# Retention attention and two mixtures of experts on one core: where weight halves are split around the last picks, one couple's transposes ahead of a weight copy, and the last block scaled by one engine

## The chip, the cores and the metric

The kernel runs on one NeuronCore of a Trainium2 chip. The metric is the device time of one execution in microseconds (us); lower is better. The engines are named as in the profile: PE (TensorE, the matrix multiplier; PEld is its loading of stationary operands), DVE (VectorE), ACT (ScalarE), POOL (GpSimd) and SP (SyncE, which here only issues DMAs). Each engine works through its own instructions in the order in which the program issues them.

## The reference, cut to what matters

```python
x = attention(q, k, v)                       # (2, 8, 768, 64) -> 1536 tokens x 512, decayed state per head
# first layer of experts: tokens with a positive skip score, top 1 of 8
xc = x[x @ w_skip > 0];  logits = xc @ w_gate;  e_idx = argmax(logits)
gate_w = softmax(logits)[e_idx]
for e in range(8):                           # w1[e]: 512 x 1024, w2[e]: 1024 x 512
    y[mask] = gate_w[mask, None] * (relu(xc[mask] @ w1[e]) @ w2[e])
x[do_compute] = xc + y
# second layer: every token, top 1 of 8 again, with a capacity of 384 tokens for an expert
logits = x @ w_gate2;  expert_idx = argmax(logits)
out[i] = gate_w[i] * expert(expert_idx[i], x[i]) if kept else 0
```

## The kernel before, in words

Everything is float32 at the interface. A weight chunk (128 x 2048, 1 MB) is loaded by SP into one of five raw buffers `big` and then **split in halves**: for each half ACT writes `hi` (a rounded copy, line 252) and DVE writes `lo` (the rest, line 255), both 128 x 1024. PE then multiplies `hi` and `lo` parts separately, three matmuls for one product (lines 786 to 788 and 794). A raw buffer is free for the next load when `lo` of its second half is done. The chunks come in a fixed order: for the first layer `w1a`, `w2a` of experts 0 to 7, then `w1b`, `w2b` of experts 0 to 7. Up to eleven halves can be held ready.

The schedule is written by hand. PE's stream is a row of steps, and after most of them the program calls `step_side()`. That moves the generators in the list `side` one step on and then calls `pump(1, pieces[0])`, which splits at most `pieces[0]` halves and issues what loads can start. `site()` moves the generators in the list `sited` one step on. So the number in `pieces[0]` decides beside which step a half is split, and the order of `site()` and `step_side()` decides what stands first on ACT and DVE.

In the first layer the loop runs over the experts `e`: `layer1` of expert `e` (x @ w1a, eight groups of matmuls into `s`), `layer2` of expert `e-1` (into `o`), and in between `turned`, which transposes on PE (line 765) into a buffer `t` and splits the result over ACT and DVE (lines 378 and 379: `xh`, `xl`, or `hTh`, `hTl`). There are three buffers `t`, used in turn, so a transposing step waits until the one three places before it has been read by both engines.

When an expert's rows are done (`result`, line 849, writes `row`), its tokens must be routed to the second layer's experts. `route_b` does that for the couples (0, 1), (2, 3) and (4, 5), for expert 6 and for expert 7. Its steps: transpose the rows (PE line 870, ACT copies `x2t`, line 871); logits (PE line 875, ACT `lgs`); the **pick** on DVE (`mx`, `d`, `t`, `tm`, `m`, lines 301 to 317); PE ranks the picked tokens (line 329); DVE makes of the ranks the slots and a one-hot matrix (`prb`, `slb`, `whereb`, lines 901 to 907); PE adds the tokens' numbers into the table `tab` (line 343).

Expert 7's pick is the last one, and it runs while PE does block (0, 0), the first 128 tokens of the second layer's expert 0, whose rows have been fetched before. Its thirteen small steps are numbered `i`; expert 7's `route_b` is moved on at `i` in (2, 4, 5, 8, 12), and at every third `i` there is a `step_side()`. Then DVE casts `tab` to `ids_b` (line 1078), and POOL gathers with it the rows of the next blocks from DRAM by indirect DMAs (line 362), block (0, 1) first. PE transposes that block's rows into `x` (line 765, `rowc`) inside `layer2` of block (0, 0). Before the change nothing is split in this stretch: `pieces[0]` is 0 there.

After that each expert has two blocks of 128 tokens, worked as a pair (lines 786 to 788). `emit_out` scales a finished block by the gate (line 919, `y`) and scatters it to the output by an indirect DMA (line 924). For the very last block alone ACT scales the left half and DVE the right half (line 921).

Of the kernel before, what the change touches and what calls it, by code (L numbers as in the profile page):

```python
# [11 lines left out]
ACTF = mybir.ActivationFunctionType  # L12
ALU = mybir.AluOpType
# [3 lines left out]
NT, DM, E, FF = B * S, H * D, 8, 1024  # L17
# [7 lines left out]
GCOL, IDCOL = DM, DM + 2  # L25
# [16 lines left out]
def kernel(  # L42
# [12 lines left out]
    nc = tc.nc  # L55
# [130 lines left out]
    def whole(kind, e, j):  # L186

        return kind == "w2a" and e in (1, 3) and j == 1
# [81 lines left out]
    def pump(n, pieces):  # L270

        count["turn"] += 1
        for _ in range(pieces):
            if not splitting:
                if not ready():
                    break
                splitting.append(split_half(n))
            try:
                next(splitting[0])
            except StopIteration:  # L280
                splitting.clear()
        load_w()
# [74 lines left out]
    def gather(at, n=None, t=None):  # L357

        n = n or done[0]
        if t is None:  # L360
            t = xs_free.pop(0)
        nc.gpsimd.indirect_dma_start(
            out=t, out_offset=None, in_=table[0:n, :], in_offset=bass.IndirectOffsetOnAxis(ap=at, axis=0),
            bounds_check=n - 1, oob_is_err=False,
        )
        return t
# [378 lines left out]
    def psum(tag="t", bufs=3):  # L745
        return ps.tile([128, 512], F32, tag=tag, bufs=bufs, name=tag)
# [13 lines left out]
    def turned(src, g, tag, divided=True):  # L760

        pool = x_p if tag == "x" else m_p
        t = psum()
        for k in range(4):
            nc.tensor.transpose(t[:, 128 * k:128 * k + 128], src[:, 512 * g + 128 * k:512 * g + 128 * k + 128], ident)
        t = t.rearrange("p (k t) -> p k t", k=4)
        if divided:
            w = 128 if tag == "x" else 256
            hi = pool.tile([128, 4, w], F32R, tag=tag + "h", name=tag + "h")[:, :, 0:128]
            lo = pool.tile([128, 4, w], F32R, tag=tag + "l", name=tag + "l")[:, :, 0:128]  # L770
            split(t, hi, lo)
            return hi, lo
        as_is = pool.tile([128, 4, 128], F32, tag=tag + "w", name=tag + "w", bufs=1)
        nc.scalar.activation(out=as_is, in_=t, func=ACTF.Copy)
        return (as_is,)

    def split_T(src, n, tag, divided=(True, True)):
        parts = []
        for g in range(n // 4):
            parts.append(turned(src, g, tag, divided[g]))  # L780
            yield
        return parts

    def mm3(acc, a, w, first, last):

        nc.tensor.matmul(out=acc, lhsT=a[0], rhs=w[0], start=first, stop=False)  # L786
        nc.tensor.matmul(out=acc, lhsT=a[0], rhs=w[1], start=False, stop=False)  # L787
        nc.tensor.matmul(out=acc, lhsT=a[1], rhs=w[0], start=False, stop=last)  # L788
# [12 lines left out]
    def layer1(x, kind, e, parts=None, fine=False):  # L801

        h = m_p.tile([128, FF], F32, tag="h", name="h", bufs=1)
        for j in range(2):
            acc = psum("s", 2)
            for k in (0, 2):
                w = wt[kind, e, j][k // 2]
                for _ in mm3s(acc, [(at_k(x, k + i), at_k(w, i)) for i in range(2)], k == 0, k == 2):
                    if fine:
                        yield  # L810
                if done_with(kind, e):
                    used((kind, e, j), k // 2)
                if not k:
                    if j and parts is not None:
                        parts.append(turned(h, 0, "hT"))
                    yield
            nc.scalar.activation(out=h[:, 512 * j:512 * j + 512], in_=acc, func=ACTF.Relu)
            yield
        return h
# [93 lines left out]
            to_slots(where[i], rhs[:, i], 8, 8)  # L913
        yield

    def emit_out(xs, acc, shared=False):
        y = m_p.tile([128, DM], F32, tag="y", name="y")
        n = DM // 2 if shared else DM
        nc.scalar.activation(out=y[:, 0:n], in_=acc[:, 0:n], func=ACTF.Copy, scale=xs[:, GCOL + 1:GCOL + 2])  # L919
        if shared:  # L920
            nc.vector.tensor_scalar(out=y[:, n:DM], in0=acc[:, n:DM], scalar1=xs[:, GCOL + 1:GCOL + 2], scalar2=None, op0=ALU.mult)  # L921
        ix = sm.tile([128, 1], I32, tag="ixo", name="ixo")
        nc.gpsimd.tensor_scalar(out=ix, in0=xs[:, IDCOL:IDCOL + 1], scalar1=4096.0, scalar2=None, op0=ALU.add)
        new = nc.gpsimd.indirect_dma_start(  # L924
            out=out[:, :], out_offset=bass.IndirectOffsetOnAxis(ap=ix, axis=0), in_=y, in_offset=None,
            bounds_check=NT - 1, oob_is_err=False,
        )
        for old in written:
            tc.declare_no_dep(new.ins, old.ins, reason="rows of other tokens")
        written.append(new)  # L930
        if xs is not a0:
            xs_free.append(xs)
# [18 lines left out]
    pieces = [1]  # L951

    def site():

        for g in list(sited):
            try:
                next(g)
            except StopIteration:
                sited.remove(g)

    def step_side():
        for g in list(side):
            try:
                next(g)
            except StopIteration:
                side.remove(g)
        pump(1, pieces[0])

    def run(gen):

        while True:
            try:
                next(gen)
            except StopIteration as stop:
                return stop.value
            step_side()
# [5 lines left out]
    def last_step(gen, n):  # L982

        for i in range(n):
            next(gen)
            if i < n - 1:
                step_side()
        try:
            next(gen)
        except StopIteration as stop:  # L990
            return stop.value

    def then_route(e, acc, between=lambda: None):

        result(e, xs1[e], acc)
        between()
        if e % 2 and e < E - 2:
            sited.append(route_b([e - 1, e], 1, 0))
        elif e == E - 2:
            side.append(route_b([e], 0, 0))  # L1000
# [15 lines left out]
    acc = run(second)  # L1016
    then_route(0, acc)
    for e in range(1, E):
        first = layer1(x, "w1a", e)
        if e == 1:  # L1020
            for _ in range(2):
                next(first)
                step_side()
            x = turned(xs1[2], 0, "x")
        h = run(first)
        if e + 4 < E:
            xs1[e + 4] = gather(ids[:, e + 4:e + 5], 1 + NT)
        elif e == 4:
            gather(ids[:, 8:9], 1 + NT, a0)
        turn = split_T(h, FT, "hT", (True, not whole("w2a", e, 1)))  # L1030
        if e > 1:
            second = layer2(hT.pop(e - 1), "w2a", e - 1)
            next(second)
            step_side()
            site()
            x = turned(xs1[e + 1] if e + 1 < E else a0, 0, "x")
            if e == E - 1:

                for _ in range(2):
                    next(second)  # L1040
                    step_side()
                    site()
                    next(turn)
            acc = last_step(second, FT // 2 - (3 if e == E - 1 else 1))
            then_route(e - 1, acc, step_side)
        if e < E - 1:
            site()
        hT[e] = run(turn)
    side += sited
    second = layer2(hT.pop(E - 1), "w2a", E - 1)  # L1050
    for i in range(FT // 2):
        next(second)
        pieces[0] = i < 2
        if i < FT // 2 - 1:
            step_side()
    acc = run(second)
# [4 lines left out]
    xs2 = {(0, 0): a0}  # L1061
# [6 lines left out]
    for i in range(1, 13):  # L1068
        next(first)
        if i % 3 == 0:  # L1070
            step_side()
        if i in (2, 4, 5, 8, 12):
            next(last)
# [14 lines left out]
    acc = run(second)  # L1088
# [44 lines left out]
    def pair_layer2(hs, e):  # L1133
        acc = [psum("o", 2), psum("o", 2)]
        for c in range(2):
            w = wt["w2b", e, c]
            for j in range(2):
                for k in range(4):
                    mm3(acc[j], at_k(hs[c], k, slice(128 * j, 128 * j + 128)), at_k(w[k // 2], k % 2), c + k == 0, c + k == 4)
                if c:  # L1140
                    emit_out(xs2[e, j], acc[j], e == E - 1 and j > 0)
                for h in range(2 * j):
                    used(("w2b", e, c), h)
                step_side()
# [11 lines left out]
    acc = run(second)  # L1156
# [207 lines left out]
```

## Time and profile before

| | |
|---|---|
| median of 3 runs | 385.44 us (385.2 to 385.46) |
| the profiled execution | 384.92 us |
| its span, first to last instruction | 383.1 us |
| PE busy | 368.7 us, 96% of the span |
| DVE, ACT, POOL busy | 64%, 56%, 32% |
| mean granted TensorE clock | 0.995 |

The profile is of one execution. The times in its rows count from the start of the span. Busy shares are means over stages with different limits: attention up to some 75 us, the first layer's experts up to some 190 us, the second layer's after that.

### The profile page before, as it was taken

Reading aid. Unit: us, or ns where it says so; the run is one execution under the profiler, and the core shown is the slowest. Engines: PE = TensorE matmul, PEld = TensorE weight load, DVE = VectorE, ACT = ScalarE, POOL = GpSimd, SP = SyncE. Lnnn points to the kernel's source line nnn. Section 1 sums busy time; section 2 is a strip of 40 time slices with the busy share of each in tenths; the row PEclk is TensorE's granted clock in tenths of the full one; section 3 lists DMA queues with packets and bytes.
Section 4 is the critical chain, followed back from the end, with each engine's and each line's share of the span. In section 5 each row is a group of like instructions: output and inputs, shape, how many; then the busy total and the mean of one; then the engine's idle time right before and its main releaser. Section 6 shows DMA issues by size and latency. Waiting matters only on the chain. (4 is left out here: it accounts for less than half of the span.)

```text
span 383.1 us, 6796 instructions
## 1 busy us (share of the span) xinstructions
PE 368.7 (96%) x2641; PEld 311.0 (81%) x2642; DVE 244.7 (64%) x402; ACT 213.8 (56%) x317; POOL 121.1 (32%) x185
## 2 busy tenths in 40 slices
PE   8999999799999999999999999999999999999992
PEld 4788887587777787886678998989899898998981
DVE  3657786479896999899626982747627466473200
ACT  1446554387986777795338763646546454562110
POOL 2677773285042060233251402205031140401102
PEclk9999999999999999999999999999999999999998
DMA  8999976689999999988746784947748386110001
GB/s 292 423 418 399 357 216 230 190 316 379 394 390 397 372 342 350 344 298 323 275 117 188 256 323 150 322 162 216 285 143 307 110 289 242 60 44 28 26 3 43
DMA packets 18128, 95.99 MB, mean 251 GB/s; under 512 B 2401, under 2 KB 2657, under 8 KB 8616
## 3 DMA queue, kind: packets, MB, share of 16 engines
q1 hardware_dynamic: 12196, 80.85, 57.2%
q0 software_dynamic: 3280, 9.76, 8.1%
q10 hardware_dynamic: 2612, 4.86, 3.5%
q8 instruction: 23, 0.38, 0.4%
q14 instruction: 17, 0.14, 0.1%
HBM read 87.03 MB, written 9.48 MB: 252 GB/s over the span
## 5 line engine op out<-in xcount | busy, mean ns | idle before, releaser
L255 DVE TENSOR_TENSOR lo<-big,hi 128x1024 fp32r<-128x1024 f32 (+1 forms) x130 | 151.3, 1185 | 54.1 <-ACT hi L252 53.6
L252 ACT ACTIVATE hi<-big 128x1024 fp32r<-128x1024 f32 (+1 forms) x130 | 128.6, 1015 | 6.9 <-DMA big<-in_w1a_dram 4.0
L788 PE MATMUL s<-xh,lo 128*128 128x256 f32 x224 | 63.4, 283 | 0.0
L787 PE MATMUL s<-xl,hi 128*128 128x256 f32 x224 | 63.4, 283 | 0.0
L786 PE MATMUL s<-xh,hi 128*128 128x256 f32 x224 | 63.4, 283 | 0.0
L924 POOL DMA_INDIRECT out_dram<-y,ixo x16 | 18.6, 1165 | 138.6 <-ACT y L919 136.6
L786 PE MATMUL o<-hi,hTh 128*128 128x512 f32 x112 | 44.2, 394 | 0.0
L788 PE MATMUL o<-hi,hTl 128*128 128x512 f32 x112 | 43.6, 390 | 0.0
L787 PE MATMUL o<-lo,hTh 128*128 128x512 f32 x112 | 43.6, 389 | 0.0
L786 PEld LDWEIGHTS s<-xh,hi 128*128 128x128 f32 x224 | 43.0, 192 | 0.3
L787 PEld LDWEIGHTS s<-xl,hi 128*128 128x128 f32 x224 | 43.0, 192 | 0.3
L788 PEld LDWEIGHTS s<-xh,lo 128*128 128x128 f32 x224 | 43.0, 192 | 0.0
L1124 ACT ACTIVATE hTh<-s 128x512 fp32r<-128x512 f32 x28 | 16.7, 598 | 39.0 <-PE s L788 39.0
L1125 DVE SCALAR_TENSOR_TENSOR hTl<-s,hTh 128x512 fp32r<-128x512 f32 x28 | 19.3, 690 | 28.4 <-ACT hTh L1124 28.4
L919 ACT ACTIVATE y<-o,rowc 128x512 f32<-128x512 f32 (+1 forms) x15 | 10.1, 675 | 45.6 <-issue 29.3
L794 PE MATMUL s<-hi,xh 128*128 128x512 f32 x80 | 32.6, 408 | 0.9 <-DVE xl L379 0.9
L794 PE MATMUL s<-lo,xh 128*128 128x512 f32 x80 | 31.3, 391 | 0.0
L794 PE MATMUL o<-hi,hTh 128*128 128x512 f32 x72 | 29.7, 412 | 0.0
L794 PE MATMUL o<-lo,hTh 128*128 128x512 f32 x72 | 28.2, 391 | 0.0
L794 PE MATMUL s<-hi,xl 128*128 128x512 f32 x80 | 25.0, 394 | 0.0
L788 PEld LDWEIGHTS o<-hi,hTl 128*128 128x128 f32 x112 | 21.0, 188 | 4.4
L787 PEld LDWEIGHTS o<-lo,hTh 128*128 128x128 f32 x112 | 21.1, 188 | 4.2
(162 smaller groups left out, 604.0 us busy)
## 6 DMA issues: line engine op xcount, KB each, us to landing
big<-in_w1a_dram SPq DMA_DIRECT2D x16, 1024.0 KB, 8.8
big<-in_w2a_dram SPq DMA_DIRECT2D x16, 1024.0 KB, 7.1
big<-in_w1b_dram SPq DMA_DIRECT2D x16, 1024.0 KB, 5.4
big<-in_w2b_dram SPq DMA_DIRECT2D x16, 1024.0 KB, 6.0
qk<-in_qkv_dram SPq DMA_DIRECT2D x5, 1024.0 KB, 9.8
big<-in_qkv_dram SPq DMA_DIRECT2D x5, 1024.0 KB, 11.7
table<-rowc ACTq DMA_DIRECT2D x5, 516.0 KB, 6.5
table<-row ACTq DMA_DIRECT2D x3, 516.0 KB, 5.5
```

Of the source, the lines that this page charges most:

```text
L252: nc.scalar.activation(out=hi[:, k], in_=r3[:, k], func=ACTF.Copy)
L255: nc.vector.tensor_tensor(out=lo[:, k], in0=r3[:, k], in1=hi[:, k].bitcast(F32), op=ALU.subtract)
L786: nc.tensor.matmul(out=acc, lhsT=a[0], rhs=w[0], start=first, stop=False)
L787: nc.tensor.matmul(out=acc, lhsT=a[0], rhs=w[1], start=False, stop=False)
L788: nc.tensor.matmul(out=acc, lhsT=a[1], rhs=w[0], start=False, stop=last)
L794: nc.tensor.matmul(out=acc, lhsT=a, rhs=w, start=first and i == 0, stop=last and i == len(todo) - 1)
L919: nc.scalar.activation(out=y[:, 0:n], in_=acc[:, 0:n], func=ACTF.Copy, scale=xs[:, GCOL + 1:GCOL + 2])
L924: new = nc.gpsimd.indirect_dma_start(out=out[:, :], out_offset=bass.IndirectOffsetOnAxis(ap=ix, axis=0), in_=y, in_offset=None, bounds_che ...
L1124: nc.scalar.activation(out=hi[:, g:g + 2, :], in_=acc, func=ACTF.Relu)
L1125: nc.vector.scalar_tensor_tensor(out=lo[:, g:g + 2, :], in0=acc, scalar=0.0, in1=hi[:, g:g + 2, :].bitcast(F32), op0=ALU.max, op1=ALU.subtract
```

## The change

Three edits. First, around the picks: in the loop's last turn (`e == E - 1`) the second of two calls of `step_side()` splits nothing, in the layer that follows one half less is split, and in block (0, 0) a half is split at `i` = 6, 9 and 12 and at the two steps of `layer2` behind them, where none was. Second, in the turn `e == 3` `site()` is called ahead of `step_side()`. Third, `emit_out` always scales with ACT alone.

```diff
-    def emit_out(xs, acc, shared=False):
+    def emit_out(xs, acc):
         y = m_p.tile([128, DM], F32, tag="y", name="y")
-        n = DM // 2 if shared else DM
-        nc.scalar.activation(out=y[:, 0:n], in_=acc[:, 0:n], func=ACTF.Copy, scale=xs[:, GCOL + 1:GCOL + 2])
-        if shared:
-            nc.vector.tensor_scalar(out=y[:, n:DM], in0=acc[:, n:DM], scalar1=xs[:, GCOL + 1:GCOL + 2], scalar2=None, op0=ALU.mult)
+        nc.scalar.activation(out=y, in_=acc, func=ACTF.Copy, scale=xs[:, GCOL + 1:GCOL + 2])
...
-            step_side()
-            site()
+
+            for step in (site, step_side) if e == 3 else (step_side, site):
+                step()
             x = turned(xs1[e + 1] if e + 1 < E else a0, 0, "x")
             if e == E - 1:
 
-                for _ in range(2):
+
+                for pieces[0] in (1, 0):
                     next(second)
                     step_side()
                     site()
                     next(turn)
+                pieces[0] = 1
             acc = last_step(second, FT // 2 - (3 if e == E - 1 else 1))
...
         next(second)
-        pieces[0] = i < 2
+        pieces[0] = i < 1
         if i < FT // 2 - 1:
             step_side()
...
         next(first)
         if i % 3 == 0:
+            pieces[0] = i > 3
             step_side()
         if i in (2, 4, 5, 8, 12):
             next(last)
...
-                    emit_out(xs2[e, j], acc[j], e == E - 1 and j > 0)
+                    emit_out(xs2[e, j], acc[j])
```

PE's, POOL's and SP's instructions keep their order. On ACT, in the turn `e == 3` (`hi` are weight copies, `x2t` the first couple's rows, `xh` the next expert's):

```order
 L817 ACTIVATE h<-s 128x512
 L252 ACTIVATE hi<-big_88 128x1024
-L252 ACTIVATE hi<-big_89 128x1024
 L871 ACTIVATE x2t<-t 128x512 x2
+L252 ACTIVATE hi<-big_89 128x1024
 L378 ACTIVATE xh<-t 128x512
 L252 ACTIVATE hi<-big_89 128x1024
```

The two copies `x2t` now stand ahead of one weight copy, of the first half of buffer 89.

On DVE, ahead of expert 6's pick (it begins with `mx` of 128x1; `prb` to `whereb` ahead of it belong to the couple (4, 5)):

```order
 L903 TENSOR_REDUCE slb<-prb 128x2
 L907 TENSOR_SCALAR whereb<-iota,slb 128x257 x2
-L255 TENSOR_TENSOR lo<-big_88,hi 128x1024 x2
+L255 TENSOR_TENSOR lo<-big_87,hi 128x1024
 L301 TENSOR_REDUCE mx<-t 128x1
 L304 TENSOR_TENSOR d<-t,mx 128x8
```

One half stands ahead of this pick where two stood. (One half fewer stands likewise ahead of the couple's own pick.)

On DVE, behind expert 7's pick (its last two rows are `tm` and `m`), up to the cast that releases the gathers:

```order
 L315 TENSOR_REDUCE tm<-t_119 128x1
 L317 TENSOR_TENSOR m<-t_119,tm 128x8
+L255 TENSOR_TENSOR lo<-big_88,hi 128x1024
 L901 TENSOR_TENSOR prb<-t,m 128x8
 L903 TENSOR_REDUCE slb<-prb 128x1
 L907 TENSOR_SCALAR whereb<-iota,slb 128x257
 L379 TENSOR_TENSOR hTl<-t,hTh 128x4x128
-L1078 CAST ids_b<-tab 128x16
-L379 TENSOR_TENSOR hTl<-t,hTh 128x4x128
+L255 TENSOR_TENSOR lo<-big_88,hi 128x1024
+L255 TENSOR_TENSOR lo<-big_89,hi 128x1024
```

One `lo` now stands between the pick and the slots, and two more stand between `hTl` and the cast of `ids_b`, which follows them.

## Rows read from the trace of the kernel before

**Rows 1.** The page's part 2: PE's busy tenths in 40 slices.

```profile
PE   8999999799999999999999999999999999999992
```

**Rows 2.** Waits of PE: engine, line, waited for, us, times, longest.

```profile
PE t L870 <- DVE row L849: 0.9, 1, 0.9
...
PE t L875 <- ACT x2t L871: 0.5, 1, 0.5
```

**Rows 3.** Timeline of ACT in the turn e = 3: start, us, instruction, idle before.

```profile
118.33 1.06 ACT L252 ACTIVATE hi<-big 128x1024 fp32r<-128x1024 f32 x1 [2.94 <-DMA big<-in_w1a_dram]
119.29 1.07 ACT L871 ACTIVATE x2t<-t 128x512 f32<-128x512 f32 x2
```

**Rows 4.** Timeline of DVE at the same place.

```profile
119.42 1.23 DVE L255 TENSOR_TENSOR lo<-big,hi 128x1024 fp32r<-128x1024 f32 x1 [2.59 <-ACT hi L252]
120.88 0.69 DVE L379 TENSOR_TENSOR xl<-t,xh 128x512 fp32r<-128x512 f32 x1 [0.23 <-ACT xh L378]
```

**Rows 5.** Timeline of PE's weight loads, at two places.

```profile
121.62 0.42 PEld L765 LDWEIGHTS t<-cs,h 128*128 128x128 f32 x4 [0.23 <-DVE xl L379]
...
198.30 0.59 PEld L765 LDWEIGHTS t<-cs,rowc 128*128 128x128 f32 x4
```

**Rows 6.** Timeline of DVE ahead of expert 6's pick.

```profile
183.25 1.23 DVE L255 TENSOR_TENSOR lo<-big,hi 128x1024 fp32r<-128x1024 f32 x1 [0.29 <-ACT hi L252]
184.40 0.16 DVE L301 TENSOR_REDUCE mx<-t 128x1 f32<-128x8 f32 x1
```

**Rows 7.** Timeline of PE at two ranking steps and at expert 7's table step.

```profile
161.00 0.61 PE L794 MATMUL o<-hi,hTl 128*128 128x512 f32 x2
161.45 0.18 PE L329 MATMUL t<-m,lc 128*128 128x16 bf16 x1
...
183.35 0.28 PE L881 MATMUL t<-zsum,lgs 128*128 128x8 f32 x2
...
184.50 0.62 PE L794 MATMUL o<-hi,hTl 128*128 128x512 f32 x2
185.49 0.18 PE L329 MATMUL t<-m,lc 128*128 128x8 bf16 x1 [0.36 <-DVE m L317]
...
193.74 0.25 PE L343 MATMUL tab<-rhsb,whereb 128*128 128x8 bf16 x4
```

**Rows 8.** Timeline of ACT behind expert 7's pick: the two ReLU copies.

```profile
191.02 0.60 ACT L817 ACTIVATE h<-s 128x512 f32<-128x512 f32 x1 [0.86 <-PE s L794]
...
193.94 0.60 ACT L817 ACTIVATE h<-s 128x512 f32<-128x512 f32 x1 [0.97 <-PE s L794]
```

**Rows 9.** Timeline of DVE behind expert 7's pick.

```profile
191.12 0.17 DVE L901 TENSOR_TENSOR prb<-t,m 128x8 f32<-128x8 f32 x1 [0.31 <-PE t L330]
...
191.52 0.36 DVE L907 TENSOR_SCALAR whereb<-iota,slb 128x257 bf16<-128x257 f32 x1
...
194.03 0.17 DVE L1078 CAST ids_b<-tab 128x16 int32<-128x16 f32 x1 [0.34 <-PE tab L343]
```

**Rows 10.** Timeline of POOL: the gather of block (0, 1).

```profile
194.60 1.11 POOL L362 DMA_INDIRECT rowc<-table,ids_b  x1 [2.67 <-DVE ids_b L1078]
```

**Rows 11.** Instructions of line 362: landing of gathers at 190 to 206, then 210 to 340.

```profile
DMA to landing us min/median/max: 3.6/3.7/3.9
...
DMA to landing us min/median/max: 3.4/4.1/5.0
```

**Rows 12.** Timeline of SP's queue: the issues of weight loads from 184.

```profile
184.51 22.17 SPq L213 DMA_DIRECT2D big<-in_w1b_dram  x2
```

**Rows 13.** Timeline of ACT at the end.

```profile
373.03 0.69 ACT L919 ACTIVATE y<-o,rowc 128x512 f32<-128x512 f32 x1 [7.64 <-PE o L788]
376.04 0.48 ACT L919 ACTIVATE y<-o,rowc 128x256 f32<-128x256 f32 x1 [2.32 <-PEq L1272]
```

**Rows 14.** Timeline of DVE at the end.

```profile
376.55 0.48 DVE L921 TENSOR_SCALAR y<-o,rowc 128x256 f32<-128x256 f32 x1 [10.43 <-ACT y L919]
```

**Rows 15.** Busy time by stretch: PE, PEld, DVE, ACT, POOL, granted clock, DMA share.

```profile
379.00:379.50 0.50, 0.00 (x0) 0.00 (x0) 0.00 (x0) 0.00 (x0) 0.00 (x0) 0.91 0.20 66
```

## The prediction

> **What bounds the kernel now.** I read the page's slices first. PE is at nine tenths or more in nearly all of them, and without a gap from slice 21, about 200 us, to the last [rows 1]. So from there on a microsecond that PE loses, or has lost before, goes into the end one for one: no later wait is left to absorb it. Then I read what PE waits for. The list has ten entries, and none is for a weight half (`hi` or `lo`): the halves are always ready in time, so splitting them earlier buys PE nothing, and splitting them later costs nothing by itself. What PE does wait for is routing work that stands behind weight splits on ACT or DVE: `x2t` for 0.5 us, expert 6's row for 0.9 [rows 2], expert 6's pick for 0.36 [rows 7]. So the change is to be judged by what stands in front of what on ACT and DVE, and DVE and ACT work off their instructions in order. After PE I read the stretch around expert 7's pick on all engines, because the three added splits fall there.
>
> **First couple ahead of a weight copy.** Before, ACT holds a weight copy until its DMA has landed (118.33, after 2.94 us of idleness), and only then copies `x2t` [rows 3]; PE waits 0.5 us for that [rows 2]. After, `x2t` runs in that idle time and the wait is gone. What is late next: the second transposing step of `h` needs the `t` buffer that `xl` frees, and waits for it already before, 0.23 us, until 121.62 [rows 5]. `xl` stands on DVE behind `lo` of the same weight half, and that half still comes at 118.33, since the DMA sets it. `lo` starts at 119.42, the next DVE instruction can start 1.15 us after such a `lo` (183.25 to 184.40) [rows 4, 6], so `xl` runs from 120.57 to 121.26 instead of 120.88 to 121.57. PE goes on at 121.30 instead of 121.62: **0.32 us gained**. The bounds are 0 (the DMA lands later) and 0.74 (both waits vanish, 0.51 and 0.23). I take 0.32 because each link has its row. Nothing that follows eats it up, as no weight half is waited for.
>
> **One half less ahead of the couple (4, 5)'s pick.** PE's wait in that stage is for expert 6's row [rows 2], which DVE can write only when PE's own sum is finished; the couple's ranking stands behind that on PE. Gain 0, and nothing is lost: the half is wanted much later.
>
> **One half less ahead of expert 6's pick.** The logits are there at 183.35 + 0.28 = 183.63 [rows 7], but `mx` starts at 184.40, right behind the `lo` of 183.25 [rows 6]. Without that `lo` the pick comes 0.73 us earlier. PE's ranking step stands at 185.49. Undisturbed it starts 0.45 us after a row of two matmuls, as 161.00 to 161.45 shows, so at 184.95 [rows 7]: the wait of 0.36 us and the hand-over around it, **0.54 us gained**. The floor is the 0.36 that the row itself names.
>
> **Three halves behind expert 7's pick.** This is the dear part. The first new `lo` stands between `m` and `prb`. Its `hi` stands on ACT behind the ReLU copy of 191.02, which lasts 0.60 [rows 8]; ACT's rows overlap by about 0.1 (118.33 + 1.06 against 119.29) [rows 3], so `hi` runs from 191.52 to 192.58 and `lo` from 192.61 (hand-over 0.03, 119.39 to 119.42 [rows 3, 4]). `prb` follows 1.15 later at 193.76 instead of 191.12, and `whereb`, which ends 0.76 after `prb` begins (191.12 to 191.52 + 0.36 [rows 9]), is done at 194.52. PE wants it at 193.74 [rows 7]: PE waits about 0.8 us where it did not wait.
>
> Then DVE does `hTl` (0.6 net, as `xl` of 0.69 in rows 4 with the overlap off) from 194.43, the second `lo` from 195.03, the third from 196.18, and comes to the cast of `ids_b` at 197.33 instead of 194.03 [rows 9], **3.30 us late**. ACT does not lengthen this: its third `hi` starts behind the ReLU copy of 193.94 [rows 8] and is done by 195.6. POOL's gather of block (0, 1) moves with the cast, from 194.60 [rows 10] to 197.90. Does anything hide that? PE begins to load that block's transposes at 198.30 [rows 5], 3.70 us after the gather's issue, and gathers issued there land 3.6 to 3.9 us after theirs [rows 11]. So the slack before is about 0.1 us, and the delay goes through to PE.
>
> What the gather takes after the change the trace does not show. Before, no weight load is issued between 184.51 and some 206 [rows 12], because no raw buffer comes free; after, the second new `lo` frees one at about 196.2, so 1 MB sets out 1.7 us before the gather. Ten gathers of the later stage run beside such loads: 3.4 to 5.0 us, median 4.1; alone the least is 3.6 [rows 11]. With 3.6 PE gets its rows at 201.5, with 4.1 at 202.0, with 5.0 at 202.9, with 3.4 at 201.3. I take 4.1, since a load stands beside it: **3.7 us lost** (bounds 3.0 and 4.6). The 0.8 us of `whereb` are within this, not on top: both are counted on the same PE. The rest of that stretch (expert 0's second half of `w2b`, the second `hTl`) is done before PE comes to it.
>
> The Trainium skill, page "DMA: Bandwidth & Descriptors", section "Queues, rings and completion order", says that a DMA engine takes turns between the queues that have work, a whole packet at a time. By that rule the gather loses time to the load, and the sum takes the longer landing (+2.5 us below) and not the one alone (3.6, so +2.0). The trace agrees as far as it goes: 4.1 beside loads, 3.6 without [rows 11].
>
> **The last block.** The two halves do not run side by side: ACT ends at 376.52, DVE starts at 376.55 and ends at 377.03 [rows 13, 14]. A whole block on ACT takes 0.69 [rows 13], so it ends at 376.73: **0.30 us gained**. The scatter follows directly; there is no other work behind which this could hide. Both bounds lie within 0.05.
>
> **Sum.** 3.7 - 0.32 - 0.54 - 0.30 = +2.5 us on the profiled execution's 384.92, 387.5. That execution was 0.52 us under the median of the runs, 385.44, and a median will be compared with that one, so I forecast 388.0.
>
> **Rivals.**
>
> *The late list stays hidden (faster).* If the gather's delay did not reach PE, only the three gains would be left: -1.16 us, 384.3. It decides at the landing: with the cast at 197.33 the rows would have to be there by 198.30, 0.4 us after the gather's issue, or DVE would have to run the cast ahead of the two splits, which its order excludes. For it speaks only that one gather's landing is not in rows 10 itself. 0.06.
>
> *The two sides balance.* The loss would have to be about 1.2 us, less than half of the least that rows 11 allow. That needs a cast that comes 1.5 us earlier than my chain, for instance if the splits cost DVE less there. 0.06.
>
> *PE's clock falls in the gap (slower still).* PE stands still for about 2.9 us before the transposes, after 0.8 us shortly ahead of them. The only fall in the trace is at the end: ACT's last scaling begins at 376.04, so PE has finished by then [rows 13], and the granted clock of 379.0 to 379.5 averages 0.91 [rows 15], a mean of full speed, 2.4 GHz, and a short piece at 1.2. If it falls here too, PE works at half rate for a while. No row shows matmuls at the low level; as an estimate, if it lasts as long as the 3.5 us at the end of the span (379.5 to 383.1), PE loses half of that, 1.8 us: 389.8. Against it: PE's other waits, 0.9 us and less [rows 2], left the clock alone, and the gap is shorter than the time from 376.04 to 379.0. The Trainium skill, page "TensorE: Matmul & The Clock Gate", section "What's actually happening", says that the array's clock is halved when PE has been idle and comes back with sustained work; the trace's end agrees, no run here shows it inside a kernel. 0.08.
>
> *The forecast.* 0.80, with its own range 387.2 to 389.0 (landing 3.4 to 5.0 and 0.1 us for the gains).
>
> **How the numbers follow.** Runs of this kernel spread by 0.26 us, so about 0.2% (0.8 us) is what can be told from no change. Slower: forecast and clock, 0.88. Same: the balance, 0.06. Faster: 0.06. The range goes from 386.5 (landing as alone, the full 0.74 for the couple) to 389.9 (the clock falls); the first two rivals are left out of it.
>
> **What would show it.** In the profile after: no wait of PE for `x2t` in the turn e = 3 but one of about 0.45 us for `xl`; none for expert 6's `m`; a wait of about 0.8 us at `tab` for `whereb`, and one of 2.5 to 3.5 us at the transposes of block (0, 1) for its gather; a cast of `ids_b` some 3.3 us later against PE's table step of 193.74 less PE's wait; one scaling of 0.69 at the end. From 205 us on PE should be as dense as before. The forecast is wrong if the transposes of block (0, 1) do not wait, or if PE waits for weight halves that it never waited for.

## The result, and the profile after

The changed kernel takes 389.22 us (median of 11 runs, 387.49 to 390.09), the kernel before 386.08 beside it (11 runs, 384.27 to 388.83). The ratio is 1.0063, with a 95% interval of 1.0034 to 1.0093: slower by about 2.4 us, between 1.3 and 3.6 (the two medians alone lie 3.1 apart). Every ratio in this document leaves out runs more than 1.5% above the fastest of their kernel, among them one of e2 at 2030.65 us and the profiled runs of e4 and e7, while the medians count them. The profiled execution took 389.7 us, its span 387.8, its mean granted clock 0.982.

The page's slices of PE, and under them those of the clock it was granted:

```profile
PE   7999999899998999999969999999999999999992
...
PEclk9799999999999999999998999999999999999997
```

The slice that begins at 194 us has fallen from nine tenths to six [rows 1]. That is the stretch around block (0, 1). The second slice of the clock row, at 10 us, shows another fall, in attention, ahead of all that was changed. It stands in six of the ten profiles of this study in some measure and not in the other four, so whole spans of single profiles are not compared below, only local stretches.

What PE waits for (engine, tile and line, waited for, us in total, times, longest):

```profile
PE t L765 <- DMA rowc<-table,ids_b: 2.4, 1, 2.4
...
PE t L765 <- DVE xl L379: 1.2, 1, 1.2
...
PE tab L343 <- DVE whereb L907: 0.7, 1, 0.7
...
PE t L870 <- DVE row L849: 0.4, 1, 0.4
```

Against [rows 2] the wait for `x2t` is gone, the one for expert 6's `row` has shrunk from 0.9 to 0.4, and behind attention three are new: for `xl`, for `whereb`, and for the rows of block (0, 1).

DVE behind expert 7's pick (start, us, instruction, idle time before it and what ended it):

```profile
192.68 1.22 DVE L255 TENSOR_TENSOR lo<-big,hi 128x1024 fp32r<-128x1024 f32 x1 [1.79 <-ACT hi L252]
193.82 0.16 DVE L901 TENSOR_TENSOR prb<-t,m 128x8 f32<-128x8 f32 x1
...
194.21 0.36 DVE L907 TENSOR_SCALAR whereb<-iota,slb 128x257 bf16<-128x257 f32 x1
194.48 0.68 DVE L379 TENSOR_TENSOR hTl<-t,hTh 128x512 fp32r<-128x512 f32 x1
195.08 2.35 DVE L255 TENSOR_TENSOR lo<-big,hi 128x1024 fp32r<-128x1024 f32 x2
197.35 0.17 DVE L1079 CAST ids_b<-tab 128x16 int32<-128x16 f32 x1
```

The gather of block (0, 1) on POOL, then the weight load on SP's queue ahead of it:

```profile
197.79 1.11 POOL L362 DMA_INDIRECT rowc<-table,ids_b  x1 [5.90 <-DVE ids_b L1079]
```

```profile
196.32 3.67 SPq L213 DMA_DIRECT2D big<-in_w1b_dram  x2
```

PE at the ranking step of expert 6, at expert 7's table step and at block (0, 1):

```profile
185.12 0.62 PE L794 MATMUL o<-hi,hTl 128*128 128x512 f32 x2
185.58 0.18 PE L329 MATMUL t<-m,lc 128*128 128x8 bf16 x1
...
194.63 0.26 PE L343 MATMUL tab<-rhsb,whereb 128*128 128x8 bf16 x4 [0.67 <-DVE whereb L907]
...
198.96 0.61 PE L794 MATMUL o<-hi,hTl 128*128 128x512 f32 x2
201.96 0.63 PE L765 MATMUL t<-cs,rowc 128*128 128x128 f32 x4 [2.38 <-DMA rowc<-table,ids_b]
```

The transposes of block (0, 1) before:

```profile
198.53 0.60 PE L765 MATMUL t<-cs,rowc 128*128 128x128 f32 x4
```

From the table step to the transposes PE needs 7.33 us; before it was 4.79 (193.74 [rows 7] to 198.53). What follows is in the stretches (length, busy us and count of PE, PEld, DVE, ACT and POOL, granted clock, DMA share, GB/s):

```profile
202.00:203.00 1.00, 1.00 (x7) 0.92 (x8) 0.00 (x0) 0.38 (x1) 0.87 (x1) 0.94 1.00 377
203.00:204.00 1.00, 1.00 (x4) 0.81 (x3) 0.69 (x1) 0.22 (x1) 0.69 (x2) 0.50 0.87 357
204.00:205.00 1.00, 1.00 (x5) 0.48 (x5) 0.11 (x1) 0.19 (x1) 0.67 (x2) 0.50 0.99 347
205.00:206.00 1.00, 1.00 (x3) 0.81 (x3) 0.07 (x1) 0.50 (x1) 0.00 (x0) 0.50 1.11 400
206.00:207.00 1.00, 1.00 (x5) 0.78 (x5) 0.00 (x0) 0.00 (x0) 0.64 (x1) 0.85 0.72 276
```

PE counts as fully busy in all five, yet from 203 on it does only 3 to 5 matmuls in each microsecond. The clock says why: behind the wait it drops to 0.50, which is 1.2 GHz instead of 2.4, until a little past 206. The busy shares alone would not have shown this.

The end, on ACT:

```profile
378.01 0.69 ACT L918 ACTIVATE y<-o,rowc 128x512 f32<-128x512 f32 x1 [7.64 <-PE o L788]
381.02 0.69 ACT L918 ACTIVATE y<-o,rowc 128x512 f32<-128x512 f32 x1 [2.32 <-PEq L1273]
```

So the account by matched instructions, after minus before: block (0, 0)'s first matmul 185.75 to 185.85, +0.10; the table step +0.89; the transposes of block (0, 1) +3.43; the last block's scaling (376.04 [rows 13] to 381.02) +4.98; the last scatter (377.81 to 382.49) +4.68. The two steps in the middle are the list: +3.33 us. The next is the clock: +1.55, of which half of some 3.2 us at 0.50 accounts for 1.6. The last is the tail: -0.30.

### The profile page after: what moved, and what is told of

Read it like the earlier page. It is cut to its first block, busy times and chain, and to the rows that moved or that the text cites. A ratio compares the mean times of both kernels' runs of the same rounds, so it can differ in the third digit from the quotient of the medians.

```text
span 387.8 us, 6795 instructions
## 1 busy us (share of the span) xinstructions
PE 370.8 (96%) x2642; PEld 313.2 (81%) x2642; DVE 244.0 (63%) x401; ACT 213.8 (55%) x317; POOL 118.6 (31%) x185
## 5 line engine op out<-in xcount | busy, mean ns | idle before, releaser
L918 ACT ACTIVATE y<-o,rowc 128x512 f32<-128x512 f32 x15 | 10.3, 689 | 45.6 <-issue 29.3
```

The costliest lines, as they stand in the source:

```text
L918: nc.scalar.activation(out=y, in_=acc, func=ACTF.Copy, scale=xs[:, GCOL + 1:GCOL + 2])
```

## The experiments

The theory: the late list costs all, 3.3 us and the clock's fall behind it, and the other edits gain 1.2 to 1.7. The rivals: the fewer halves ahead of the picks or the couple's new order do harm; the clock costs nothing in time; the loss lies in `whereb`, or in the halves' number, and not in the cast.

**e1_behind_cast**: the changed kernel, with the three halves behind the cast of `ids_b`.

```diff
         if i % 3 == 0:
-            pieces[0] = i > 3
             step_side()
...
         load_block(e, j)
+    pieces[0] = 1
+    step_side()
     second = layer2(h0, "w2b", 0)
```

> The changed kernel, but nothing is split between expert 7's pick and the cast of ids_b; two halves follow right behind the cast and the rest after. Theory (the late cast is the loss): PE waits neither for whereb nor for the gather of block (0, 1), the cast stands right behind the table step, the granted clock stays 1.00 around 200 us, and what is left of the change is its gains: 0.54 us at expert 6's pick, 0.5 at expert 6's row (its wait fell from 0.92 to 0.39), 0.3 at the end and about 0.3 at the first couple, so about 1.7 us faster than before (ratio 0.994 to 0.998) and 3 to 5 us faster than the changed kernel. Rival (the two halves taken away ahead of the picks are missing later): PE waits for a weight half of expert 0's w2b at 197 to 199 us, and the time is that of before or worse.

384.67 us (12 runs) against 385.46 (33); ratio 0.9985 (0.9958 to 1.0012). PE in its trace:

```profile
192.34 0.26 PE L343 MATMUL tab<-rhsb,whereb 128*128 128x8 bf16 x4
...
197.13 0.60 PE L765 MATMUL t<-cs,rowc 128*128 128x128 f32 x4
```

4.79 us again, as before, with no wait at either place, and a clock of 1.00 from 196 to 205. With the halves split some 3 us later against PE's work, both waits are gone. So they hung on the place of the halves against the cast, and not on anything earlier in the change. The profiled span is 381.4, 1.7 under that of before; the runs put the gain at 0.6 us, anywhere from 1.6 faster to 0.5 slower. That is less than the 1.7 expected, which lies just outside.

**e2_one_early**: e1, and one half split right behind expert 7's `result`, ahead of its pick.

```diff
     result(E - 1, xs1[E - 1], acc)
+    pieces[0] = 1
     step_side()
+    pieces[0] = 0
     last = route_b([E - 1], 0, 0)
```

> As e1_behind_cast, and one of the two halves is split between expert 6's row and expert 7's pick, where DVE and ACT stand idle for some 2.4 us. Theory: that half is free there (no PE wait near 187 to 191 us), and expert 0's second w2b half is ready earlier, so the same time as e1_behind_cast or up to 0.3 us less. Rival: the lo of 1.23 us pushes the pick of expert 7 back, PE waits up to 1 us at its ranking step, and it is slower than e1_behind_cast by that.

383.3 us (12 runs), ratio 0.9943 (0.991 to 0.9975): the fastest version here by its median, 2.2 us under the kernel before. DVE there:

```profile
185.43 1.22 DVE L255 TENSOR_TENSOR lo<-big,hi 128x1024 fp32r<-128x1024 f32 x1
187.84 0.17 DVE L301 TENSOR_REDUCE mx<-t 128x1 f32<-128x8 f32 x1 [1.18 <-PE t L881]
```

The half costs nothing: behind it DVE still stands idle for 1.18 us until PE has the logits. In e1, without the half, DVE stands idle for 2.31 us at the same place. The span of e2, 381.3, is e1's (381.4), so the 1.4 us between the two medians is not seen in the profiles and is not claimed for the half.

**e3_dummies**: the changed kernel, with nine matmuls of zeros ahead of the transposes of block (0, 1), into a buffer that these then overwrite.

```diff
-    x = turned(xs2[0, 1], 0, "x")
+    x = turned(xs2[0, 1], 0, "x", dummies=9)
```

> The changed kernel with nine 128x512 bf16 matmuls of zeros on PE ahead of the transposes of block (0, 1), about 2 us of work in the 2.4 us wait; nothing else differs. Theory (the clock fell because PE stood still): the wait for the gather shrinks to about 0.4 us, the transposes begin at the same place as in the changed kernel, the granted clock stays 1.00 from 200 to 207 us, and the time is about 1.5 us under the changed kernel's. Rival (the slow stretch of 203 to 206 us comes from the DMAs or from something else): the clock falls there as well and the time is that of the changed kernel.

387.81 us (12 runs), ratio 1.0043 (1.0015 to 1.0072): 0.8 us under the changed kernel by the two ratios, 1.4 by the two medians, where 1.5 was expected. PE, then the stretches:

```profile
199.72 2.12 PE L550 MATMUL t<-zb 128*128 128x512 bf16 x9
202.24 0.66 PE L766 MATMUL t<-cs,rowc 128*128 128x128 f32 x4 [0.40 <-DMA rowc<-table,ids_b]
...
205.67 0.39 PE L795 MATMUL s<-hi,xh 128*128 128x512 f32 x1
```

```profile
202.00:204.00 2.00, 1.76 (x10) 1.44 (x10) 0.44 (x1) 0.60 (x1) 1.39 (x3) 1.00 0.95 387
204.00:206.00 2.00, 2.00 (x12) 1.57 (x11) 0.44 (x2) 0.69 (x1) 1.11 (x3) 1.00 0.97 373
```

The transposes come no sooner: 7.32 us behind the table step (194.92), the changed kernel's 7.33. But the clock stays at 1.00, and the 12 matmuls of 204 to 206 stand against 8 in the changed kernel's rows. The same matmul as the last row above, in the changed kernel:

```profile
206.90 0.39 PE L794 MATMUL s<-hi,xh 128*128 128x512 f32 x1
```

From the transposes to it PE needs 3.43 us here (202.24 to 205.67) and 4.94 in the changed kernel (201.96 to 206.90). So the gap and the clock are two separate losses, and the second is some 1.5 us. The intervals of the two kernels' ratios overlap, so the time alone would not prove it; these rows do.

**e4_late_cast**: the kernel before, with ten additions of zero to `iota` ahead of the cast. No half is moved and no weight load set off; this adds work to DVE.

```diff
+    for _ in range(10):
+        nc.vector.tensor_scalar(out=iota, in0=iota, scalar1=0.0, scalar2=None, op0=ALU.add)
     nc.vector.tensor_copy(out=ids_b, in_=tab[:, 8:24])
```

> The kernel before, with ten in-place additions of zero to the 128x257 table iota on DVE ahead of the cast of ids_b (some 3 us), and no weight half moved, so no load beside the gather. Theory (the cast's lateness alone): the cast comes some 3 us later, the gather lands about 3.6 us after its issue, PE waits some 3 us at the transposes of block (0, 1), the clock falls behind that wait in most executions, and the time is 3 to 5 us over before. Rival (the 1 MB load beside the gather is what hurts): the wait is under 1 us.

388.94 us (10 runs), ratio 1.0073 (1.0041 to 1.0105): 2.8 us slower, between 1.6 and 4.0, where 3 to 5 were expected. A late cast alone makes the kernel before about as slow as the change does. DVE, POOL, PE and the clock:

```profile
198.61 3.26 DVE L1079 TENSOR_SCALAR iota<-iota 128x257 f32<-128x257 f32 x10
201.79 0.17 DVE L1080 CAST ids_b<-tab 128x16 int32<-128x16 f32 x1
```

```profile
202.24 1.11 POOL L362 DMA_INDIRECT rowc<-table,ids_b  x1 [5.30 <-DVE ids_b L1080]
```

```profile
198.73 0.25 PE L343 MATMUL tab<-rhsb,whereb 128*128 128x8 bf16 x4
...
205.88 1.08 PE L765 MATMUL t<-cs,rowc 128*128 128x128 f32 x4 [2.20 <-DMA rowc<-table,ids_b]
```

```profile
204.00:206.00 2.00, 0.12 (x1) 0.15 (x2) 0.00 (x0) 0.00 (x0) 1.65 (x2) 0.97 0.68 178
206.00:208.00 2.00, 2.00 (x7) 1.75 (x8) 0.37 (x1) 0.60 (x1) 1.44 (x2) 0.50 0.73 215
```

From the table step to the cast it is 3.06 us, before 0.29 (193.74 to 194.03 [rows 7, 9]): 2.77 late. To the transposes it is 7.15 instead of 4.79: 2.36 lost. The difference, 0.4, is the slack that the list had before, and by it the wait is 2.20 us and not the 3 expected. No load moves between 200 and 204 here (DMA share 0.00 in that stretch), and the gather's rows are at PE 3.64 us after its issue.

**e5_split6** and **e6_split9_12** take the three halves apart: in block (0, 0) e5 splits only at `i` = 6, e6 only at 9 and 12.

```diff
-            pieces[0] = i > 3
+            pieces[0] = i == 6    # e5; and pieces[0] = 1 behind the load_block calls
+            pieces[0] = i > 6     # e6
```

> The changed kernel with the first of its three halves kept (the lo between expert 7's pick and its slots) and the other two moved behind the cast. Theory (each DVE row in front delays what stands behind it by its length, and the gather has about 0.4 us of slack): PE waits 0.6 to 0.7 us for whereb as in the changed kernel, the cast comes about 1.0 us late instead of 3.3, no load stands beside the gather, it lands 3.6 us after its issue and PE waits for it 0 to 0.2 us; the clock stays 1.00; the time is about 0.9 us under before. Rival (the cast matters, whereb does not): PE's wait for whereb is absorbed and the time is that of e1_behind_cast.

> The changed kernel with the split at i = 6 left out: two lo stand between hTl and the cast, none in front of the slots. Theory: no wait for whereb; the cast comes about 2.7 us late; the gather lands about 4.1 us after its issue, since the second lo frees a raw buffer whose load sets out ahead of it; PE waits 2.5 to 3.0 us in one piece and the clock falls behind that wait; the time is 1.5 to 4 us over before. Rival (the three splits share the loss evenly): a wait of some 1.6 us at most and no fall of the clock.

e5: 385.49 us (10 runs), ratio 1.0004 (0.9973 to 1.0035). That holds both no change and the 0.9 us expected. e6: 390.52 us (only 4 runs), ratio 1.0115 (1.0053 to 1.0177), so 4.4 us slower, between 2.0 and 6.8, where 1.5 to 4 were expected. PE of e5, then the cast, gather and PE of e6:

```profile
194.33 0.26 PE L343 MATMUL tab<-rhsb,whereb 128*128 128x8 bf16 x4 [0.67 <-DVE whereb L907]
```

```profile
198.79 0.17 DVE L1079 CAST ids_b<-tab 128x16 int32<-128x16 f32 x1
```

```profile
199.24 1.11 POOL L362 DMA_INDIRECT rowc<-table,ids_b  x1 [5.16 <-DVE ids_b L1079]
```

```profile
204.84 1.09 PE L765 MATMUL t<-cs,rowc 128*128 128x128 f32 x4 [4.02 <-DMA rowc<-table,ids_b]
```

The split at 6 costs the 0.67 us for `whereb` and nothing behind it: in e5 the transposes start 4.79 us after the table step, without a wait. The splits at 9 and 12 cost no wait for `whereb`, but the whole of the gather's. Their cast is 2.62 late against PE's table step (0.29 before, 2.91 here); the changed kernel's is 3.2 late against a table step without the wait for `whereb`. Yet PE waits 4.02 us, where 2.5 to 3.0 were expected, so in these two traces two halves ahead of the cast cost more than three do: it is not their number. Missed was the landing: 5.60 us from issue to PE. In e6 SP issues the next 1 MB load at 198.90, 0.34 us ahead of the gather; in the changed kernel it was 1.47 ahead (196.32 to 197.79), and the gather took 4.17. That the start of the load makes the difference was not tried apart. The clock then lies at 0.50 from 203.2, before the wait ends, to 210.0.

**e7_copy_first** and **e8_x_first**: e2 with other orders in the turn `e == 3`; e7 as before the change, e8 with the weight copy behind `site()` and the transposes of `x` both.

```diff
-            for step in (site, step_side) if e == 3 else (step_side, site):
-                step()
+            step_side()               # e7
+            site()
             x = turned(xs1[e + 1] if e + 1 < E else a0, 0, "x")
...
+            if e != 3:                # e8
+                step_side()
+            site()
             x = turned(xs1[e + 1] if e + 1 < E else a0, 0, "x")
+            if e == 3:
+                step_side()
```

> e2_one_early with the first couple's edit undone: the weight copy stands ahead of x2t again. Theory: PE waits for x2t again (0.5 us or more, since the copy waits for its DMA), and from that DMA's landing to the second transposes of h it takes 3.29 us as in the kernel before instead of 2.97, so it is 0.3 us slower than e2_one_early, less than the timing can tell. Rival (the edit saves the whole wait): 0.7 us or more slower than e2_one_early.

> e2_one_early with the weight split of that step behind x as well: x2t, then xh and xl, then the half. Theory (xl stands behind the late lo, which gives most of the couple's gain back): PE waits neither for x2t nor for xl there, and it comes to the second transposes of h 0.7 to 1.2 us earlier than in e2_one_early, counted from the transposes of the couple's rows; the time is as much under e2_one_early's, 0.5% to 0.9% under before. Rival (the DMAs set that stage anyway): PE waits for a weight half or for another copy a few us later and the time is that of e2_one_early.

e7: 384.31 us (12 runs), ratio 0.995 (0.9918 to 0.9981). e8: 383.94 (12 runs), 0.9955 (0.9918 to 0.9993). In time neither can be told from e2 (0.991 to 0.9975). As expected, in e7's trace PE waits 1.97 us for `x2t`, and its second transposing step starts 3.30 us after the weight copy (120.73 to 124.03); in e2 this is 2.98. Behind that wait the clock of e7 falls:

```profile
122.00:124.00 2.00, 1.18 (x12) 0.58 (x12) 1.74 (x2) 2.00 (x4) 0.00 (x0) 0.97 1.00 418
124.00:126.00 2.00, 2.00 (x8) 1.78 (x8) 1.77 (x2) 2.00 (x3) 0.00 (x0) 0.50 0.98 414
126.00:128.00 2.00, 2.00 (x7) 1.58 (x7) 2.00 (x3) 2.00 (x5) 0.00 (x0) 0.68 0.89 258
```

The edit moves the couple's logits into PE's wait and shortens it, so it might be worth more than its 0.32 when the landing is late; no run shows that. In e6, which has the edit, PE waited 2.15 us for `xl` there, and the clock of 126 to 128 is 0.50 as well. In e8 both waits of the couple are gone: counted from the transposes of the couple's rows, PE is at the sum behind the second transposes 1.28 us sooner than in e2 (6.95 against 8.23). But PE pays at its ranking instead, as the rival said:

```profile
PE t L329 <- DVE m L317: 1.3, 1, 1.3
```

The couple's pick now stands on DVE behind a row of `lo`, whose `hi` wait for their DMAs (2.29, 1.11 and 1.02 us of ACT's idleness between 119 and 128). What this order of ACT and DVE won against the DMA came back one step later.

## Why the prediction was right, and where it was off

**The list behind expert 7's pick: right, step by step.** Forecast was a wait for `whereb` of 0.8 us (measured 0.67), the cast at 197.33 (197.35), the gather at 197.90 (197.79), a landing of 4.1 (4.17 to PE), and 3.7 us lost in all (3.33). The 0.4 of difference is the slack before, put at 0.1 and measured at 0.4 by e4. It was read from the least gather, 3.6 [rows 11], against the start of PE's weight loads, but PE would not have needed the rows then: its own sums lasted longer. That the 0.8 lies within the loss and not on top held too: the two waits of the changed kernel, 0.67 and 2.38, make 3.05 of the 3.33. e5 has the 0.67 alone and no wait behind it. e1 shows that the place does it, e4 that the cast alone is enough.

**The landing beside a load: right in the changed kernel.** It took 4.17 us beside a load, 3.64 without one (e4). The prediction cited the Trainium skill, page "DMA: Bandwidth & Descriptors", section "Queues, rings and completion order", for queues that take turns by packets; the runs agree in direction. How much it costs varies: in e6, where the load started closer to the gather, it took 5.60, which the forecast's upper bound, 5.0, did not cover.

**One half less ahead of the couple's pick: the step that failed.** It was put at "Gain 0", because DVE could write expert 6's row "only when PE's own sum is finished". PE's sum was finished. Its last matmuls start at 176.50 and the next sum at 176.96, and DVE writes the row at 178.53, some 1.6 us later: the row stood in DVE's order behind the `lo` of 175.52, the couple's whole pick and `hTl`, and DVE had no idle time in between (PE and DVE before):

```profile
176.50 0.62 PE L794 MATMUL o<-hi,hTl 128*128 128x512 f32 x2
```

```profile
175.52 1.21 DVE L255 TENSOR_TENSOR lo<-big,hi 128x1024 fp32r<-128x1024 f32 x1
...
177.93 0.69 DVE L379 TENSOR_TENSOR hTl<-t,hTh 128x512 fp32r<-128x512 f32 x1
178.53 0.74 DVE L849 SCALAR_TENSOR_TENSOR row<-o,rowc 128x512 f32<-128x512 f32 x1
```

Without that `lo` (DVE and PE after):

```profile
178.55 0.69 DVE L379 TENSOR_TENSOR hTl<-t,hTh 128x512 fp32r<-128x512 f32 x1 [0.51 <-ACT hTh L378]
179.16 0.74 DVE L849 SCALAR_TENSOR_TENSOR row<-o,rowc 128x512 f32<-128x512 f32 x1
```

```profile
179.05 0.61 PE L794 MATMUL o<-hi,hTl 128*128 128x512 f32 x2
180.05 0.63 PE L870 MATMUL t<-cs,row 128*128 128x128 f32 x4 [0.39 <-DVE row L849]
```

PE's wait fell from 0.92 to 0.39, a gain of 0.53, which e1 and e2 show alike. What is left is no longer DVE's order: DVE waits 0.51 us for ACT's `hTh`, and ACT had itself stood idle 0.62 us for PE. The wait's name ("for row") said who came last, not why; the idle time ahead of that DVE row, which is none in the kernel before, would have told that DVE was busy without a break.

**One half less ahead of expert 6's pick: right.** 0.54 us forecast. The ranking step now follows its matmuls by 0.46 us without a wait, as from 161.00 to 161.45 [rows 7].

**First couple ahead of a weight copy: right by 0.32, wrong in what the wait would read.** From the weight copy (its DMA's landing) to the second transposing step it was 3.29 us before (118.33 to 121.62 [rows 3, 5]), and is 2.97 after (119.83 to 122.80). With the edit it is 2.97 or 2.98 in five experiments, without it 3.30 in e7. But PE's wait for `xl` was forecast at about 0.45 and is 1.19, since the landing itself came at 119.83 instead of 118.33; it moves from profile to profile (118.06 in e2, 120.98 in e8). The 0.32 is below what the runs can tell. What the clock adds when the landing is late (e7) was not in the forecast.

**The last block on ACT alone: right.** From ACT's last scaling to the scatter it was 1.77 us (376.04 to 377.81), and is 1.47 (381.02 to 382.49): 0.30.

**The clock's fall: a rival at 0.08 that came true in the profiled execution.** Its price, 1.8, was near the 1.55 that the trace gives. The case against it leaned on the end of the trace [rows 15] and on shorter waits, and neither held for this one. The Trainium skill's page "TensorE: Matmul & The Clock Gate", section "What's actually happening", says that idleness halves the clock; the stretches of the changed kernel and of e4 now show it inside this kernel, and e3 shows that work in the gap prevents it.

**The sum.** By the trace it is -0.32 - 0.53 - 0.54 - 0.30 + 3.33 + 1.55 = +3.2 us; the runs say +2.4, between 1.3 and 3.6; forecast was +2.5. The missed gain of 0.53, the loss that was 0.4 smaller and the clock's fall offset each other in part, so the total came out closer than its terms, and that much of it was luck. How often the clock falls so stays open. The mean clocks of the 11 runs reach from 0.981 to 0.998; as 3.2 us at 0.50 take 0.004 off the mean of a span of 388, the run at 0.998 (388.29 us) had no such fall and is still 2.2 us above the median before. Of the others the mean does not say, since falls in attention and at the end are in it too.

**The range and the noise.** The lower end of the range, 386.5, was worked out from the profiled execution's 384.92 (3.2 - 0.74 - 0.54 - 0.30 = +1.6); from the median, 385.44, on which the forecast stands, it would be 387.1. And the spread of 0.26 us came from three runs; the eleven beside the change reach over 4.6 us (384.27 to 388.83), so 0.8 us was less than a few runs can tell.

## What to carry to other kernels

When work of no urgency is pushed behind the last link of a chain, ask what follows that link on the same engine: here a cast of 0.17 us released a gather with 0.4 us of slack, and three weight halves ahead of it cost 3.3 us, while behind it they cost nothing. When the profile says that PE waits for a DVE result, look at the idle time ahead of that DVE instruction before naming the cause: none means that the engine was still busy with what stands ahead, and taking something out there can be a gain (here 0.53 us for a half of 1.2). And price a PE gap with the clock behind it: look at the granted clock for the microseconds after it, since busy shares hide a half-speed stretch.

## What the runs showed of the hardware that was not expected

- The clock fell to 0.50, for some 3 us each time, behind single waits of 1.97 us (e7), 2.15 (e6), 2.20 and 2.61 (e4, the second for `x2t`) and 2.38 (the changed kernel). Behind the wait of 4.02 (e6) it lay there for 6.8 us. It stayed at 1.00 behind waits of 1.19 (the changed kernel) and 1.31 (e5) for `xl`. At the end of the kernel before it had stayed up longer after PE's last work, from 376.04 to 379.0 at the least [rows 13, 15].
- The same 128-row gather was at PE 3.64 us after its issue alone, 4.17 with a 1 MB load issued 1.47 us ahead, and 5.60 with one issued 0.34 us ahead. The second of these is repeated by e3 (4.15), the other two are single executions. The fourth gather of the list, issued at 202.13 in the changed kernel, landed 6.6 us after its issue, with no one waiting for it; the least of this list before was 3.6 [rows 11].
- A fall of the clock near the start was in part absorbed. In the profile of the changed kernel it averages 0.76 from 6 to 20 us, where the kernel before has 1.00; a matmul of line 401 comes 1.47 us later (16.47 to 17.94), but a matmul of line 829 only 0.55 later (103.15 to 103.70). What takes up the difference was not tried.
